# Two transformer layers on one core: the zero-padded queries made by DMA instead of by masked copies on VectorE, value matmuls of shifted copies listed one by one, and a newly planned order

## The chip, the cores and the metric

The kernel runs on one core of a Trainium2 chip. Five engines work side by side, each through its own list of instructions in the order written: TensorE (PE, matmuls), VectorE (DVE), ScalarE (ACT), GpSimd (POOL) and SyncE (SP, which issues the DMAs). They wait for each other by semaphores. The metric is the device time of one execution in microseconds (us); lower is better.

## The reference

Two layers, each an attention block and a dense block, over 2048 tokens of 512 numbers with 32 heads of 16. All data are bfloat16, and both layers use the same weights.

```python
def _A_ref(x, wqkv, wo):            # 32 heads, Dh = 16
    qkv = (x @ wqkv).reshape(B, S, 3, H, Dh)...
    scores = jnp.einsum("bhqd,bhkd->bhqk", q, k) * (Dh ** -0.5)
    p = softmax(scores)
    o = jnp.einsum("bhqk,bhkd->bhqd", p, v)
    return o.reshape(B, S, D) @ wo
def _B_ref(x, w1, b1, w2, b2):      # F = 1792
    return gelu(x @ w1 + b1) @ w2 + b2
x = x + _A_ref(layernorm(x), A_wqkv, A_wo)
x = x + _B_ref(layernorm(x), B_w1, B_b1, B_w2, B_b2)
# and both lines once more
```

Most of the work is in the scores: 2 layers x 32 heads x 2048 x 2048 exponentials, and the matmuls on both sides of them.

## The kernel before, in words

**Cells and passes.** The unit of attention is a cell: 128 keys by 512 query columns for one head (or, in the last two segments, 256 columns for each of two heads). A score matmul multiplies a 32-row slice of K (two heads of 16) with a 32-row slice of the padded query, `QP`, in which the 16 rows of the other head are zero. Slice a of four works on rows 32a to 32a+31 of TensorE, so up to four cells run at the same time. `passes` (L1211) cuts the 4096 cells into 96 passes: a pass is one padded query (half of the heads of a block of 128 rows, one segment of columns) with 16, 32, 48 or 64 cells. In the first layer the first segment's keys are taken in two parts, in the second layer those of the first two segments in three (`PARTS`, L50), which gives 24 passes of only 16 cells.

**Two ways to an exponential.** Most cells go to ACT: one ACTIVATE (L1751) takes two cells, sometimes three, from PSUM to the tiles `pt` (which, late or early, also lie in parts of K, Q, V and G that are free: these show up as `kt`, `q`, `v`, `g` at L1751). The others, at most those of 5 key tiles in 16 (`KD`), go to VectorE: one TENSOR_SCALAR (L1507) makes from the score a 16-bit word that, read as bfloat16, is roughly the exponential, and POOL makes three shifted copies of a pair of such cells with two integer adds (L1596 one copy, L1598 two). Each of the four copies is multiplied with its own scaled copy of V (`VC`) and all are added in PSUM: an exact enough exponential costs PE four value matmuls where one of ACT's cells costs one. Value matmuls (L1817) go in rounds of up to four, one for each column group a. The buffers `DU` of such pairs are few (5, and up to 5 lent ones).

**The padded query.** `QP` has three slots of 512 columns. `qpad` (L1288) makes one for each pass but the first: it waits for a slot, and VectorE multiplies the block of Q by a column of zeros and ones (L1299, 128x512 for most passes; two 128x256 ones for each of the last 8). The slot is given back when all scores of its pass have been handed out.

**Other work.** Loads of weights, `wr` (L1035), transposes of LayerNorm tiles by DMA (L778) and moves of x (L690) are all on SP's queue. VectorE also empties the projections from PSUM, adds residuals (L983, L1132), does LayerNorm (L734 to L774) and normalizes attention (L919 to L955). Projections and dense matmuls are L607.

**The order.** Nothing is ordered by hand. `_Sched` (L251) is a list scheduler that runs while the program is built: it keeps a clock for each engine, a cost for each operation, the time at which each result is ready (with a latency by engine, for a DMA a `tail`), and pools of buffers and PSUM banks. Generators yield operations; the one that can start first, or among those ready the one with the best priority, is taken, and the wait instructions follow from what it reads and writes. A VectorE operation marked as `port` starts, in the planner's eyes, only after the POOL operation that is running (`_ready`, L329), and POOL's after it. Whether a score group gets one more cell for VectorE is decided as PE's group is issued (`attach`, L1435): there must be a free bank, a free `DU` buffer, and VectorE's planned clock must not be too late. If none is attached, ACT may get a third cell (`extend`). Every 24 us of planned ACT time (`STRETCH`) ten settings of the planner are exchanged: `PICKS` names one of the rows of `ORDERS` for each stretch. Where PE would idle, it gets a filler matmul (L1339), and incomplete rounds get multiplications by zero (L1825).

Two places that a sentence cannot give are these, of the padded query and of the list of value matmuls (entries of `dq` are in the order in which PE will take them):

```python
s = yield ("acq", "qp")
for i, t in enumerate(ts):
    yield _Op("dve", 0.15 + 0.262 * w / 512, ... tensor_scalar(T["QP"][:, s, w*i:w*i+w], q, T["MASK"][:, t:t+1], 1.0, ...
...
yield _Op("pool", ..., words(2, 2), words(0, 2), 2 * SHIFT * ONES), ...)
self.chains -= 1
for jj, (pi, kt, a) in enumerate(cells):
    for i in range(4):
        self.dq[(pi, a)].append(...)
```

Of the kernel before, what the change touches and what calls it, by code (L numbers as in the profile page):

```python
# [27 lines left out]
QP_RING = 3  # L28
W_RING = 4
# [88 lines left out]
class _Prog:  # L118
# [72 lines left out]
    def group(self, eng, fns, reads=(), writes=(), sem=None, by=1):  # L191
        if sem is None:
            sem = ENG_SEM[eng]
        self._dep_waits(eng, reads, writes)
        for i, fn in enumerate(fns):
            last = i == len(fns) - 1
            self.prog[eng].append(("do", fn, sem if last else None, by if last else 0))
# [22 lines left out]
class _Op:  # L220
    __slots__ = ("eng", "cost", "fns", "reads", "writes", "sem", "by", "tail", "prio", "mode", "slack", "late", "back", "port", "limit", "after")

    def __init__(self, eng, cost, fns, reads=(), writes=(), sem=None, by=1, tail=0.0, prio=None, mode="F", slack=None):
        self.eng, self.cost = eng, cost
        self.fns = fns if isinstance(fns, list) else [fns]
        self.reads, self.writes = list(reads), list(writes)
        self.sem, self.by, self.tail, self.prio, self.mode, self.slack = sem, by, tail, prio, mode, slack
        self.limit = 1e9
        self.late, self.after = None, []
        self.port = eng == "dve" and self.writes[:1] != [] and self.writes[0].startswith(("OTT", "NMR", "QP", "VC", "XLN", "PT", "V0", "V1")) and not self.reads[:1] == [] and not self.reads[0].startswith("B.")  # L230
# [20 lines left out]
class _Sched:  # L251
# [23 lines left out]
    def route(self, name, what):  # L275
        return name
# [205 lines left out]
def bass_interleave_layers__mha_block__dense_activation_gelu__prompt_kernel(  # L482
# [15 lines left out]
    with ExitStack() as es:  # L498
# [28 lines left out]
        if DU % 2:  # L527
# [31 lines left out]
                     "dout", "dk0", "dk1"] + ["dwr%d" % i for i in range(W_RING + W_MORE)] + ["dtr%d" % i for i in range(XLN_RING)]  # L559
# [37 lines left out]
class _Plan:  # L597
# [12 lines left out]
    def init(self):  # L610
# [16 lines left out]
        yield _Op("dve", 0.6, lambda e: e.memset(self.bank(PVB), 0.0), writes=["B.%d" % PVB])  # L627
        yield _Op("dve", 0.1, lambda e: e.tensor_reduce(
# [170 lines left out]
    def proj(self, l, kind, i, c, src, skeys, ph, done):  # L799
# [43 lines left out]
        if (l, kind, i, c) == (0, "Q", 0, 0):  # L843
            s = yield ("acq", "qp")
            self.hold.add(b)
            yield _Op("dve", DV, lambda e: e.tensor_scalar(T["QP"][:, s, :], pb, T["MASK"][:, 0:1], None, op0=ALU.mult),
                      reads=["B.%d" % b, "MASK"], writes=["QP.%d" % s, "QFIRST"])
            first = ["QFIRST"]
            yield ("give", ("qp", 0), s)
# [437 lines left out]

    def qpad(self):  # L1288
        T = self.T
        for pi, (l, seg, g, kts, part, final) in enumerate(self.pas):  # L1290
            if pi == 0:
                continue
            b, ts = self.heads(seg, g)
            qc, q0, w = seg
            yield ("need", ("Q", l, b, qc))
            s = yield ("acq", "qp")
            q = T["Q"][:, b, 512 * qc + q0:512 * qc + q0 + w]
            for i, t in enumerate(ts):
                yield _Op("dve", 0.15 + 0.262 * w / 512, lambda e, s=s, q=q, i=i, t=t, w=w: e.tensor_scalar(  # L1299
                    T["QP"][:, s, w * i:w * i + w], q, T["MASK"][:, t:t + 1], 1.0, op0=ALU.mult, op1=ALU.mult),  # L1300
                    reads=["Q.%d.%d" % (b, qc), "MASK"], writes=["QP.%d" % s])
            yield ("give", ("qp", pi), s)
# [39 lines left out]
    def score(self, cell, qs, bank):  # L1342

        T = self.T
        pi, kt, a = cell
        l, seg, g = self.pas[pi][:3]
        gb = self.heads(seg, g)[0]
        lhsT = T["K"][l][32 * a:32 * a + 32, gb, kt * 128:(kt + 1) * 128]
        rhs = T["QP"][32 * a:32 * a + 32, qs, :]
        o = self.bank(bank)  # L1350
        return (lambda e: e.matmul(o, lhsT=lhsT, rhs=rhs, start=True, stop=True, tile_position=(32 * a, 0)),  # L1351
                ["K%d.%d.%d" % (l, gb, kt // 4), "QP.%d" % qs])
# [9 lines left out]
    def next_d(self, used, start, pop=True):  # L1362
        tok = self.s.tokens
        for pi in (self.pa, self.pa + 1):
# [12 lines left out]
            for k, (_, kt, a) in enumerate(self.dlist[pi]):  # L1377
                if a not in used and ("vc", l, kt) in tok and ("K", l, gb, kt // 4) in tok:
                    r = ["K%d.%d.%d" % (l, gb, kt // 4), "QP.%d" % tok[("qp", pi)]]
# [78 lines left out]
    def scores(self):  # L1458
        u = 0
        pools = self.s.pools  # L1460
        while True:
# [25 lines left out]
            for d, b, pair, j in extra:  # L1487
                yield ("spawn", self.dfirst(pair, j, b), DPRIO)
                if j == 0:
                    yield ("spawn", self.dchain(pair), CPRIO)  # L1490
# [14 lines left out]
    def dfirst(self, pair, j, b):  # L1505
        u = self.T["DU"][pair["du"]][:, 0, j, :]
        yield _Op("dve", 0.682, lambda e: e.tensor_scalar(u, self.bank(b), E_SCALE, E_BIAS, op0=ALU.mult, op1=ALU.add),  # L1507
                  reads=["B.%d" % b], writes=["DU.%d.0.%d" % (pair["du"], j)] + self.over(pair["du"]))
        pair["done"] = pair.get("done", 0) + 1
        yield ("rel", "dbank", b)  # L1510

    def solo(self):
# [10 lines left out]
        while True:  # L1523
# [10 lines left out]
            yield ("spawn", self.dfirst(pair, j, b), DPRIO)  # L1534
# [43 lines left out]
    def dchain(self, pair):  # L1578
# [9 lines left out]
        n = len(cells)  # L1588
        U = T["DU"][du]
        key = [["DU.%d.%d.%d" % (du, i, j) for j in range(n)] for i in range(4)]  # L1590
        def words(i, k):
# [5 lines left out]
                  reads=key[0], writes=key[1])  # L1597
        yield _Op("pool", 0.143 + 0.4352 * n, lambda e: e.int64_add(words(2, 2), words(0, 2), 2 * SHIFT * ONES),  # L1598
                  reads=key[0] + key[1], writes=key[2] + key[3])
        self.chains -= 1  # L1600
        self.duleft[du] = n
        for jj, (pi, kt, a) in enumerate(cells):
            l, seg, g = self.pas[pi][:3]
            gb, ts = self.heads(seg, g)
            j = KD[l].index(kt)
            for i in range(4):
                if i == 0:
                    ws, wk = [T["V"][l][:, kt, 8 * gb + 2 * a + t, 0:17] for t in ts], ["V%d.%d" % (l, kt), self.vone(l, kt)]
                else:
                    ws = [T["VC"][:, j, i - 1, 17 * h:17 * h + 17] for h in [8 * gb + 2 * a + t for t in ts]]  # L1610
                    wk = ["VC.%d.%d" % (j, i - 1)]
                self.dq[(pi, a)].append((ws, U[:, i, jj, :].bitcast(BF16), wk + [key[i][jj]],
                                         ("du", du) if i == 3 else None, i == 3, kt))
# [247 lines left out]
    def run(self):  # L1861
# [10 lines left out]
        s.pool("qp", range(QP_RING))  # L1872
# [54 lines left out]
```

## Time and profile before

| | |
|---|---|
| median of 3 runs | 1480.15 us (1477.9 to 1480.68) |
| the profiled execution | 1478.68 us |
| its span, first to last instruction | 1476.7 us |
| TensorE clock granted | 0.999 |
| VectorE exponents (L1507) | 858 + 200 + 115, mean 0.682 to 0.683 us |
| ACT exponentials (L1751) | 1164 of two cells, 198 of three, 1 of one |
| POOL adds (L1596, L1598) | 607 and 607 |
| masked copies (L1299) | 87 of 512 columns, 16 of 256 |
| DMA, all queues | 103.35 MB, 70 GB/s in the mean |

A row of the groups reads: line, engine, operation, what it writes and reads, shape, how many, then busy time and the mean of one in ns, then the idle time of the engine before them and who ended it. Busy time of ACT and PE counts overlapping instructions from start to end, so their steps are shorter than their durations. The windows' rows give the stretch in us, its length, then busy time and number for the engine asked, the granted clock, the DMA engines' share and GB/s.

### The profile page before, as it was taken

The page shows a single profiled execution, that of the slowest core. Times are in us where ns is not written, and L with a number is a line of the kernel's source. Part 1 is how long each engine was busy: PE and PEld are TensorE (multiplying, and loading weights), DVE is VectorE, ACT ScalarE, POOL GpSimd, SP SyncE. Part 2 cuts the span into 40 slices and gives each one's busy share as a digit, 9 for nine tenths or more (in the row PEclk, how much of TensorE's full clock was granted, in tenths as well). Part 3 has the DMA queues.
Part 4 walks back from the last instruction along what each step waited for, and adds up shares of the span by engine and source line. Part 5 has one row for each costly group of instructions (what it writes and reads, how often), then busy time and mean ns, then how long its engine had stood idle before and what let it go on. Part 6 is the DMA issues. An engine that isn't in the chain of part 4 may idle for free.

```text
span 1476.7 us, 45759 instructions
## 1 busy us (share of the span) xinstructions
PE 1415.5 (96%) x19639; PEld 428.0 (29%) x19639; DVE 1219.1 (83%) x2246; ACT 1427.6 (97%) x1422; POOL 977.8 (66%) x1235
## 2 busy tenths in 40 slices
PE   8999999999999999999999999999999999999999
PEld 3222222222222222222222222222222222334445
DVE  7768989878987789987797788999968987887683
ACT  7999999999999999999999999999999999999995
POOL 1057977867676777886556756667867876776661
PEclk9999999999999999999999999999999999999999
DMA  5200001153112521114320243101143115511533
GB/s 154 49 2 1 2 16 30 38 168 82 47 45 59 164 66 31 48 34 130 122 60 25 59 122 114 30 2 37 30 131 115 37 37 137 158 31 38 162 91 95
DMA packets 145045, 103.35 MB, mean 70 GB/s; under 512 B 37069, under 2 KB 143822, under 8 KB 144846
## 3 DMA queue, kind: packets, MB, share of 16 engines
q1 hardware_dynamic: 144846, 100.44, 24.6%
q8 instruction: 157, 2.57, 0.8%
q14 instruction: 42, 0.34, 0.1%
HBM read 88.61 MB, written 4.19 MB: 63 GB/s over the span
## 4 chain that ended last, share of the span: by engine, by line
ACT 52%; PE 30%; DVE 14%; DMA 1%; POOL 1%; issue 1%; SPq 0%; ACTq 0%; DVEq 0%
ACT pt L1751 41%; PE ps L607 10%; PE ps L1351 10%; PE ps L1817 9%; DVE du L1507 6%; ACT g L1102 3%; ACT kt L1751 2%; ACT q L1751 2%; ACT v L1751 2%; DVE kt L1507 1%; DVE v L1507 1%; DVE xln L774 1%; DVE stats L734 1%; DMA wr<-in_B_w_dram 1%; ACT L1102 1%
## 5 line engine op out<-in xcount | busy, mean ns | idle before, releaser
L1751 ACT ACTIVATE pt<-ps 128x1024 bf16<-128x1024 f32 (+1 forms) x1096 | 1103.9, 1136 | 18.2 <-PE ps L1351 12.0
L1507 DVE TENSOR_SCALAR du<-ps 128x512 uint16<-128x512 f32 x858 | 572.4, 683 | 115.9 <-PE ps L1351 112.3
L1351 PE MATMUL ps<-qp,kt 32*128 32x512 bf16 x4096 | 553.8, 384 | 37.4 <-ACT pt L1751 11.4
L1596 POOL INT64_ADD du<-du x444 | 266.9, 602 | 318.5 <-DVE du L1507 290.9
L1598 POOL INT64_ADD du<-du x444 | 449.1, 1013 | 35.5
L1817 PE MATMUL ps<-du,vc 128*17 128x512 bf16 (+1 forms) x2856 | 324.2, 360 | 1.4 <-ACT pt L1751 0.5
L1351 PEld LDWEIGHTS ps<-qp,kt 32*128 32x128 bf16 x4096 | 144.7, 91 | 601.3 <-issue 175.0
L1817 PE MATMUL ps<-pt,v 128*17 128x512 bf16 (+1 forms) x2630 | 283.9, 360 | 5.3 <-ACT pt L1751 2.1
L1507 DVE TENSOR_SCALAR kt<-ps 128x512 uint16<-128x512 f32 x200 | 134.7, 682 | 34.0 <-PE ps L1351 33.2
L1817 PE MATMUL ps<-du,v 128*17 128x512 bf16 (+1 forms) x952 | 142.4, 360 | 3.9 <-DVE xt L937 1.2
L1817 PE MATMUL ps<-kt,vc 128*17 128x512 bf16 (+1 forms) x714 | 136.3, 347 | 0.1
L607 PE MATMUL ps<-xf,wr 128*32 128x512 bf16 (+1 forms) x1888 | 131.0, 365 | 0.0
L607 PE MATMUL ps<-wr,g 128*32 128x512 bf16 x1600 | 118.9, 382 | 1.6 <-DMA wr<-in_B_w_dram 1.5
L1598 POOL INT64_ADD kt<-kt x104 | 105.1, 1011 | 8.3
L1817 PEld LDWEIGHTS ps<-du,vc 128*17 128x17 bf16 x2856 | 87.7, 89 | 75.3 <-issue 38.1
L1596 POOL INT64_ADD kt<-kt x104 | 62.4, 600 | 60.8 <-DVE kt L1507 57.4
L1817 PEld LDWEIGHTS ps<-pt,v 128*17 128x17 bf16 x2630 | 69.1, 88 | 87.7 <-issue 62.5
L1817 PE MATMUL ps<-v,vc 128*17 128x512 bf16 (+1 forms) x402 | 90.3, 350 | 0.0
L1081 DVE TENSOR_SCALAR g<-ps,hb1t 128x512 bf16<-128x512 f32 (+1 forms) x112 | 79.2, 708 | 12.7 <-PE ps L607 12.0
L1817 PE MATMUL ps<-kt,v 128*17 128x512 bf16 (+1 forms) x390 | 85.9, 360 | 1.6 <-DVE xt L937 1.3
L1507 DVE TENSOR_SCALAR v<-ps 128x512 uint16<-128x512 f32 x115 | 77.5, 682 | 11.9 <-PE ps L1351 11.6
L1751 ACT ACTIVATE kt<-ps 128x1024 bf16<-128x1024 f32 (+1 forms) x71 | 78.5, 1134 | 2.5 <-PE ps L1351 0.6
(108 smaller groups left out, 1555.4 us busy)
## 6 DMA issues: line engine op xcount, KB each, us to landing
wr<-in_B_w_dram SPq DMA_DIRECT2D x256, 256.0 KB, 2.9
wr<-in_A_wqkv_dram SPq DMA_DIRECT2D x24, 256.0 KB, 2.9
wr<-in_A_wo_dram SPq DMA_DIRECT2D x18, 256.0 KB, 3.1
x<-in_A_x_dram SPq DMA_DIRECT2D x7, 512.0 KB, 4.1
kept<-x SPq DMA_DIRECT2D x4, 512.0 KB, 2.9
x<-kept SPq DMA_DIRECT2D x4, 512.0 KB, 4.1
out_dram<-x SPq DMA_DIRECT2D x16, 128.0 KB, 2.6
g<-in_A_wqkv_dram SPq DMA_DIRECT2D x3, 512.0 KB, 6.0
```

Source lines behind the costliest of these rows:

```text
L607: return [lambda e, a=a: e.matmul(out[32 * a:32 * a + 32, :], lhsT=lhsT[:, 32 * a:32 * a + 32], rhs=rhs, start=start, stop=stop, tile_posi ...
L734: yield _Op("dve", 0.66, lambda e, t=t: e.bn_stats(T["STATS"][:, t, :], T["X"][:, t % XT, :]), reads=["X.%d" % (t % XT)], writes=["ST.%d" ...
L774: yield _Op("dve", 0.41, lambda e: e.tensor_scalar(xl, T["X"][:, t % XT, :], T["RSTD"][:, t:t + 1], T["NMR"][:, t:t + 1], op0=ALU.mult, op ...
L1081: yield _Op("dve", 0.21 + n / 966, lambda e, fc=fc, pb=pb: e.tensor_scalar(T["G"][:, fc, q], pb, T["HB1T"][:, fc:fc + 1], None, op0=ALU.ad ...
L1102: lambda e, g=g: e.activation(out=g, in_=g, func=ACT.Gelu_apprx_tanh), reads=gk, writes=gk, prio=2)
L1351: return (lambda e: e.matmul(o, lhsT=lhsT, rhs=rhs, start=True, stop=True, tile_position=(32 * a, 0)), ["K%d.%d.%d" % (l, gb, kt // 4), "Q ...
L1507: yield _Op("dve", 0.682, lambda e: e.tensor_scalar(u, self.bank(b), E_SCALE, E_BIAS, op0=ALU.mult, op1=ALU.add), reads=["B.%d" % b], writ ...
L1596: yield _Op("pool", 0.151 + 0.2176 * n, lambda e: e.int64_add(words(1, 1), words(0, 1), SHIFT * ONES), reads=key[0], writes=key[1])
L1598: yield _Op("pool", 0.143 + 0.4352 * n, lambda e: e.int64_add(words(2, 2), words(0, 2), 2 * SHIFT * ONES), reads=key[0] + key[1], writes=k ...
L1751: yield _Op("act", 0.065 + 0.4267 * n, lambda e, src=src, dst=dst: e.activation(out=dst, in_=src, func=ACT.Exp, scale=0.25), reads=["B.%d" ...
L1817: op.fns.append(lambda e, o=o, lhsT=q[0][0][m], rhs=q[0][1][:, n * m:n * m + n], a=a, st=st, sp=sp: e.matmul(o, lhsT=lhsT, rhs=rhs, start= ...
```

## The change

The wide masked copies are replaced by four DMAs on SP for each pass, 16 rows by 512 columns each, from `Q` into `QP`; the zero rows are written once at the start by a memset. For that a slot may only ever hold the same half: `QP` gets four slots, two for even and two for odd passes, each with a semaphore of its own (all four DMAs count on it, 64 in all). Keys for reads and writes are now kept for each slice a. The 256-column segments keep their copies on VectorE. Entries for value matmuls are appended singly, the unshifted copy when the exponent has been handed out, the shifted ones after each POOL add, where before all followed the second add. Small LayerNorm operations are marked as `port`, so that the planner counts on their waiting for POOL. `PICKS` is new.

```diff
-QP_RING = 3
+QP_RING = 4
...
-PICKS = (3, 9, 9, 3, 3, 3, 9, 3, 1, 3, 3, 9, 9, 9, 1, 9, 9, 3, 9, 9, 5, 3, 3, 9,
-         3, 9, 9, 9, 3, 1, 9, 9, 3, 9, 9, 9, 3, 3, 9, 3, 9, 3, 9, 9, 3, 5, 9, 5,
-         1, 9, 9, 9, 9, 3, 9, 9, 5, 3, 4, 3)
+PICKS = (3, 3, 3, 1, 3, 3, 1, 3, 4, 3, 3, 1, 3, 1, 3, 3, 4, 4, 3, 1, 3, 3, 1, 1,
+         3, 1, 1, 3, 3, 1, 1, 1, 1, 5, 1, 7, 1, 5, 3, 3, 5, 8, 3, 1, 9, 1, 1, 1,
+         3, 3, 3, 1, 3, 3, 1, 7, 3, 3, 4, 3)
...
+        spread = sem not in ENG_SEM and len(fns) > 1
...
+            if spread:
+                self.prog[eng].append(("do", fn, sem, by // len(fns)))
...
-... self.writes[0].startswith(("OTT", "NMR", "QP", "VC", "XLN", "PT", "V0", "V1")) ...
+... self.writes[0].startswith(("OTT", "NMR", "QP", "VC", "XLN", "PT", "V0", "V1", "VARR", "RSTD", "RA", "RB")) ...
...
+        yield _Op("dve", 0.5, lambda e: e.memset(T["QP"][:, 1:QP_RING, :], 0.0), writes=[k for i in range(1, QP_RING) for k in self.qkeys(i)])
...
+        if name == "qp":
+            return "qp%d" % (b % 2)
...
-            s = yield ("acq", "qp")
+            s = yield ("acq", "qp%d" % (pi % 2))
             q = T["Q"][:, b, 512 * qc + q0:512 * qc + q0 + w]
-            for i, t in enumerate(ts):
+            if w == 512:
+                fns = []
+                for a in range(4):
+                    rows = slice(32 * a + 16 * ts[0], 32 * a + 16 * ts[0] + 16)
+                    fns.append(lambda e, s=s, q=q, rows=rows: e.dma_start(T["QP"][rows, s, :], q[rows, :]))
+                yield _Op("sp", 1.6, fns, reads=["Q.%d.%d" % (b, qc)], writes=self.qkeys(s), sem="dqp%d" % s, by=64, tail=2.0)
+            for i, t in enumerate(ts) if w < 512 else ():
...
-    def dfirst(self, pair, j, b):
+    def dfirst(self, cell, pair, j, b):
...
+        self.copied(cell, pair["du"], j, 0)
...
+        self.duleft[du] = n
...
             reads=key[0], writes=key[1])
+        for jj in range(n):
+            self.copied(cells[jj], du, jj, 1)
...
             reads=key[0] + key[1], writes=key[2] + key[3])
+        for i in (2, 3):
+            for jj in range(n):
+                self.copied(cells[jj], du, jj, i)
         self.chains -= 1
-        self.duleft[du] = n
-        for jj, (pi, kt, a) in enumerate(cells):
...
+    def copied(self, cell, du, jj, i):
...
+        if i == 0:
+            ws, wk = [T["V"][l][:, kt, h, 0:17] for h in hs], ["V%d.%d" % (l, kt), self.vone(l, kt)]
+        else:
+            j = KD[l].index(kt)
+            ws, wk = [T["VC"][:, j, i - 1, 17 * h:17 * h + 17] for h in hs], ["VC.%d.%d" % (j, i - 1)]
+        self.dq[(pi, a)].append((ws, T["DU"][du][:, i, jj, :].bitcast(BF16), wk + ["DU.%d.%d.%d" % (du, i, jj)],
+                                 ("du", du) if i == 3 else None, i == 3, kt))
...
-        s.pool("qp", range(QP_RING))
+        s.pool("qp0", range(0, QP_RING, 2))
+        s.pool("qp1", range(1, QP_RING, 2))
```

More of the change, by code (lines that the diff above doesn't have):

```diff
@@ L229, in __init__ @@
         self.late, self.after = None, []
-        self.port = eng == "dve" and self.writes[:1] != [] and self.writes[0].startswith(("OTT", "NMR", "QP", "VC", "XLN", "PT", "V0", "V1")) and not self.reads[:1] == [] and not self.reads[0].startswith("B.")
+        self.port = eng == "dve" and self.writes[:1] != [] and self.writes[0].startswith(("OTT", "NMR", "QP", "VC", "XLN", "PT", "V0", "V1", "VARR", "RSTD", "RA", "RB")) and not self.reads[:1] == [] and not self.reads[0].startswith("B.")
 class _Thread:
@@ L558, in bass_interleave_layers__mha_block__dense_activation_gelu__prompt_kernel @@
         sem_names = ["pe", "act", "dve", "pool", "dxt0", "dxt1", "dxt2", "dxt3", "dx1", "dx2", "dx3", "dwq", "dwk", "dwv", "db1", "db2"] + ["dw%d" % c for c in range(3)] + [
-                     "dout", "dk0", "dk1"] + ["dwr%d" % i for i in range(W_RING + W_MORE)] + ["dtr%d" % i for i in range(XLN_RING)]
+                     "dout", "dk0", "dk1"] + ["dwr%d" % i for i in range(W_RING + W_MORE)] + ["dtr%d" % i for i in range(XLN_RING)] + ["dqp%d" % i for i in range(QP_RING)]
         sems = {n: es.enter_context(nc.semaphore("s_" + n)) for n in sem_names}
@@ L1286, in vcopies, with qkeys @@
             self.lend = 1
+    def qkeys(self, s):
+        return ["QP.%d.%d" % (s, a) for a in range(4)]
     def qpad(self):
@@ L1487, in scores @@
             for d, b, pair, j in extra:
-                yield ("spawn", self.dfirst(pair, j, b), DPRIO)
+                yield ("spawn", self.dfirst(d, pair, j, b), DPRIO)
                 if j == 0:
@@ L1533, in solo @@
             d, b, pair, j = extra[0]
-            yield ("spawn", self.dfirst(pair, j, b), DPRIO)
+            yield ("spawn", self.dfirst(d, pair, j, b), DPRIO)
             if j == 0:
```

28 lines of the change are left out of this document (12 added, 16 removed).

## The prediction

> **What bounds the kernel now.** I read the page first, for the engines' totals and the chain of work that ended last.
>
> ```profile
> span 1476.7 us, 45759 instructions
> PE 1415.5 (96%) x19639; PEld 428.0 (29%) x19639; DVE 1219.1 (83%) x2246; ACT 1427.6 (97%) x1422; POOL 977.8 (66%) x1235
> ...
> ACT 52%; PE 30%; DVE 14%; DMA 1%; POOL 1%; issue 1%; SPq 0%; ACTq 0%; DVEq 0%
> ...
> L1751 ACT ACTIVATE pt<-ps 128x1024 bf16<-128x1024 f32 (+1 forms) x1096 | 1103.9, 1136 | 18.2 <-PE ps L1351 12.0
> L1507 DVE TENSOR_SCALAR du<-ps 128x512 uint16<-128x512 f32 x858 | 572.4, 683 | 115.9 <-PE ps L1351 112.3
> ```
>
> ACT, PE and DVE all look full, so the question is which of them is out of work last. The chain of waits in order of time gives ACT's true rate, because successive exponentials overlap in the busy column:
>
> ```profile
> 195.31 2.27 ACT kt L1751 x2
> ...
> 224.83 1.15 DVE qp L1299
> ...
> 434.08 6.42 ACT pt L1751 x7
> ```
>
> Seven exponentials of two cells take 6.42 us, 0.917 each; a three-cell one shows 1.34 to 1.35 where it stands alone. Split by shape, the trace has 1164 pairs, 198 triples and one single: 1164 x 0.917 + 198 x 1.34 = 1333 us. With the gelus (47 us), the table loads (21) and small copies (14) ACT needs 1415 of 1476.7 us. The remaining 60 or so are mostly the 12.6 us ahead of the first exponential, the end after the last score (1448 us on), and waits for scores. The view of ACT's waits puts 12.0 us on PE's score matmuls in 24 waits. So **ACT is the bound**, and its work shrinks only if a cell (one head group by 128 keys) goes to VectorE instead: 2328 + 594 + 1 cells are ACT's, 858 + 200 + 115 = 1173 are VectorE's (the three L1507 groups), 4096 together. The code allows VectorE 5 of 16 key tiles, 1280 cells; 107 are still open.
>
> Where are they missing? The exponents on VectorE (L1507) by stretches of 60 us, and then the masked copies (L1299) in the same view:
>
> ```profile
> 720.00:780.00 60.00, 25.39 (x38) 1.00 0.26 67
> 840.00:900.00 60.00, 29.37 (x44) 1.00 0.46 133
> 900.00:960.00 60.00, 29.76 (x44) 1.00 0.18 50
> ...
> 840.00:900.00 60.00, 3.12 (x8) 1.00 0.46 133
> 900.00:960.00 60.00, 5.41 (x11) 1.00 0.18 50
> ```
>
> Most stretches hold 50 to 60 exponents, about the allowed share; seven after the start hold fewer (360, 720, 840, 900, 960, 1320, 1380 us: 48, 38, 44, 44, 43, 46, 49). Those seven hold 16.7 us of masked copies, 14.7 of it ahead of the 256-column segments, because the second layer's first passes are short and each pass makes one.
>
> **The change, part by part.**
>
> (1) *The masked copies leave VectorE.* By shape and from the view of the line itself:
>
> ```profile
> L1299 DVE TENSOR_SCALAR qp<-q,mask 128x512 bf16<-128x512 bf16 x87 | 39.8, 457 | 9.0 <-PE ps L1351 8.9
> ...
> L1299 DVE TENSOR_SCALAR qp<-q,mask x103: 268/344/1222, 13.3 to 1386.2; 128x512 bf16<-128x512 bf16 x87, 128x256 bf16<-128x256 bf16 x16
> ...
> 712.74 1.21 DVE L1299 TENSOR_SCALAR qp<-q,mask 128x512 bf16<-128x512 bf16 x1
> 712.76 1.04 POOL L1598 INT64_ADD du<-du  x1
> ```
>
> The 87 wide ones go, 87 x 0.457 = 39.8 us; the 16 of the two 256-column segments stay (7.4 us). The median is 0.344 and the longest 1.222: at 712.74 the copy lasts until the POOL add beside it ends, so it waits for that add. What is it worth? Bounds: nothing, if the planner finds no cell for the freed time, and 39.8 / 0.60 = 66 cells if all of it is refilled (0.60 is VectorE's back-to-back step per exponent in the chain at 211 to 224 us). I take the short stretches: 14.7 / 0.60 = 24 cells, since elsewhere the share of cells is at its limit. Each cell saves half a pair on ACT, 0.459 us: **-11 us** (bounds 0 and -30). PE does not lose by it: such a cell needs four value matmuls for one, three quarters of a 0.213 us round more (rounds of four columns follow each other at 0.21 in the timeline), 0.16 us; and it saves half a score group, which from the steady loop at 700 us (0.865 us for one score group and two rounds) costs 0.865 - 0.43 = 0.43, so 0.22.
>
> (2) *The copies on the path.* Summed over the chain, masked copies hold it for 9.8 us in 17 pieces, five of them over 1 us, as at 224.83. There exponents, LayerNorm and residual adds follow each other at 0.6 us, so VectorE itself is next and gets its work earlier; in the other pieces the next score or POOL is late at once. I take a third, **-3** (bounds 0 and -9.8), the rest being in (1) already.
>
> (3) *Four DMAs per pass on SP.* 87 x 4 = 348 more issues against about 400 in the trace. Four x loads of 128 KB take 1.82 us to issue, 0.46 each, the one-row bias load 0.24; so 1.0 to 1.8 us per pass, under 160 us on a queue whose listed work is far less than the span. Landing: 128 KB loads take 2.2 us, 512 KB ones 4.1. So a padded Q is there 4 us after its slot is free, against 0.46 now. The cover: from the end of the copy to the pass's first score there are 5.9 to 10.7 us in the 24 passes of 16 cells (868 to 1003 us), 2.2 in the pass after them, 12 to 48 elsewhere, except 6.3 and 9.9 in the first two. The slot now frees one pass earlier (two slots for each parity instead of three for all), about 5.5 us more there. **0 us**; without the cover, some 4 us per pass. In the first pass the loads keep the DMA engines full until 16 us and its scores begin at 18 to 20. The weight loads behind the DMAs on SP have margin: PE waits for them 1.5 us in all (bound +3). Every first score now also waits for a DMA semaphore; with the data landed I take nothing.
>
> (4) *Value matmuls handed out singly.* The unshifted copy of a cell can be used when its exponent is made, not after both POOL adds (0.60 and 1.01 to 1.04 us). PE waits little for POOL (1.6 us with its array idle), and POOL holds the chain for 1% of the span, 15 us, nearly all of it from 146 to 161 us where POOL itself is the limit and nothing is gained. But rounds can be filled earlier and the exponents' buffers come free sooner: **-1** (bounds 0 and -8).
>
> (5) *Waits for POOL in the plan, and the new order.* The LayerNorm steps of two or four columns now count as held up by POOL. The shortest `ra` steps take 0.14 us, the mean of the 2-column ones is 0.391; 38 of each kind with the other steps give some 20 us over their minimum. Planning cannot abolish the waits, only place them: -1. All 60 stretches get new settings: ACT's waits between exponentials, about 50 us in all, are redealt, and I see nothing that gives the sign (bounds -10 and +10), 0.
>
> (6) *Start:* one memset of 1536 columns more on VectorE, near 0.5 us (L627 takes 0.485 for 512 float32), at a time when VectorE waits for x: 0.
>
> Sum: -11 - 3 + 0 - 1 - 1 = -16; against the profiled execution, 1478.68 (span 1476.7 and 2.0 around it), 1462.7. That execution lies 1.5 under the median of the runs, 1480.15, so against the median 1464.2. Rounded up, since (1) and (2) share time, I forecast **1465 us**, 1.0% faster.
>
> **A rule that speaks against it.** The shortest landing in the trace, 2.2 us, is for 128 KB; here each transfer has 16 KB. The Trainium skill, DMA: Bandwidth & Descriptors, Rules for kernel authors, says to coalesce small transfers, since under 64 KB one pays mostly overhead. By that rule four in a row would pay it four times; were they served one after another at 2.2 us, Q would land after 9 us, still inside 5.9 + 5.5 us of the shortest lead, so it bears on the second rival's chance and not on the sum.
>
> **The rivals.**
>
> *No room.* VectorE already runs 83% and idles only while it waits for scores (112 + 33 + 12 us); if banks and the 5-of-16 limit, not its time, decide, no cells move and only (2), (4) and (5) remain, with PE (30% of the chain) next: 1478.7 - 4 and up to the time before, so 1474 to 1481, point 1477. For it: most stretches are at the share. Against it: the short stretches coincide with the masked copies. 0.22.
>
> *Late queries, slower.* SP runs in order. A padded Q stands behind transposes of LayerNorm tiles, for whose inputs SP waits up to 14.9 us at a time, and behind weight loads that wait for PE up to 161 us when the order places them early. If the real machine lags the plan, Q lands after the pass has begun, PE stops at the first score with everything queued behind it, and ACT follows within one exponential. It decides from 5.9 + 5.5 = 11.4 us between a free slot and landing. At 13 us the 24 short passes would lose 1.6 us each, 38 us over them if none is made up; halved for what ACT and VectorE have in stock, +19, less the 4 of (2) and (4): about 1494. Against it: 4 us needed, 11.4 there. 0.10.
>
> *The new order is worse.* PE's and ACT's waits grow by more than the gain, +8 after the saving: 1487. 0.08.
>
> **How the numbers follow.** Forecast case 0.60, its own range 1449 to 1474; no room 0.22; late queries 0.10; worse order 0.08. About 0.2% (3 us) is what a measurement of this kernel can tell from no change. Faster by more, under 1477: all of the forecast case and half of "no room", 0.71; within: most of its other half, 0.10; slower: the last two cases and its end at 1481, 0.19. The range, to leave out two in ten at most, goes from 1446 (66 cells at the most would give 1450 and the redealt waits the rest) to 1484.
>
> **What would show it.** Right: no wide L1299 groups on VectorE; L1507 groups sum to about 1197 (1180 to 1235); fewer ACT pairs, ACT's waits unchanged; SP's q<-q transfers landing in 2 to 4 us; no DMA of qp among PE's releasers. Wrong: as many L1507 as before, or fewer; PE idle before L1351 released by a DMA; more ACT idle from L1351; PE's zero-fills (L1825, 313) growing. What would make the forecast wrong: VectorE's freed time ending as idle while it waits for scores.

## The result: 0.23% slower

The changed kernel takes 1482.74 us in the median of 14 runs (1482.08 to 1484.64), the kernel before, run beside it, 1479.22 us (14 runs): a ratio of 1.0023, 95% interval 1.0015 to 1.0031. The forecast was 1465 us. The profiled execution took 1482.37 us with a span of 1480.6 us, 3.9 us more than before's 1476.7; the granted clock is 0.997, against 0.999 (where it fell is told below).

The page of the changed kernel: span, engines, chain of waits, the two groups of exponentials (line, engine, operation, shape, how many, then busy time and mean ns, idle time ahead and what ended it), and the DMA row of the padded queries (how many, KB each, median us to landing).

```profile
span 1480.6 us, 46284 instructions
PE 1419.3 (96%) x19765; PEld 431.6 (29%) x19765; DVE 1198.7 (81%) x2171; ACT 1421.8 (96%) x1410; POOL 986.5 (67%) x1233
...
PE 45%; ACT 37%; DVE 13%; POOL 3%; DMA 1%; issue 1%; SPq 1%; ACTq 0%; POOLq 0%; DVEq 0%
...
L1775 ACT ACTIVATE pt<-ps 128x1024 bf16<-128x1024 f32 (+1 forms) x1093 | 1100.0, 1126 | 25.0 <-PE ps L1367 13.6
L1523 DVE TENSOR_SCALAR du<-ps 128x512 uint16<-128x512 f32 x865 | 573.2, 683 | 143.1 <-PE ps L1367 139.4
...
qp<-q SPq DMA_DIRECT2D x348, 16.0 KB, 1.8
```

Lines have moved: exponents on VectorE are L1523 (L1507 before), on ACT L1775 (L1751), scores L1367 (L1351), LayerNorm outputs `xln` L779 (L774), their transposes L783 (L778); the DMAs of padded queries are L1312. The copies are gone and VectorE is busy 20.4 us less, but its idle time ahead of the exponents that wait for scores has grown from 115.9 to 143.1 us in the `du` group. The three groups hold 865 + 202 + 117 = 1184 cells, 11 more than before, and ACT is busy 5.8 us less. In the chain ACT fell from 52% to 37% and PE rose from 30% to 45%: ACT is less often the one that is late.

Where did the time go? The trace gives the time of each of the 4096 score matmuls. I divide the span at the 256th and at the last of them. For all kernels of this study, in us (the column LN is the time from `varr`, the first small operation of a LayerNorm, to `nmr`, the last, summed over the 25 LayerNorm groups):

| kernel | median | ratio to before, 95% | 256th score | from there to the last | after the last | LN | cells on VectorE |
|---|---|---|---|---|---|---|---|
| before | 1479.22 | | 117.6 | 1330.1 | 29.0 | 113.9 | 1173 |
| after | 1482.74 | 1.0023 (1.0015 to 1.0031) | 123.2 | 1322.6 | 34.8 | 137.8 | 1184 |
| e1 | 1486.41 | 1.0049 (1.0033 to 1.0065) | 122.3 | 1333.3 | 29.0 | 113.1 | 1173 |
| e2 | 1490.18 | 1.0081 (1.0068 to 1.0094) | 118.4 | 1334.2 | 34.8 | 140.8 | 1184 |
| e3 | 1478.25 | 0.9993 (0.9983 to 1.0002) | 118.1 | 1323.6 | 34.8 | 138.6 | 1184 |
| e4 | 1498.23 | 1.0123 (1.0093 to 1.0153) | 117.8 | 1337.8 | 39.4 | 115.0 | 1169 |
| e5 | 1498.68 | 1.0126 (1.0097 to 1.0156) | 119.6 | 1328.7 | 49.6 | 152.9 | 1173 |
| e6 | 1492.09 | 1.0082 (1.0053 to 1.0111) | 120.9 | 1329.6 | 38.7 | 106.1 | 1165 |
| e7 | 1490.80 | 1.0071 (1.0048 to 1.0094) | 120.7 | 1332.4 | 35.9 | 103.2 | 1177 |
| e8 | 1477.35 | 0.9983 (0.9974 to 0.9993) | 120.5 | 1326.2 | 28.9 | 107.0 | 1175 |
| e9 | 1498.62 | 1.0127 (1.0106 to 1.0148) | 120.6 | 1350.3 | 28.9 | 108.9 | 1175 |
| e10 | 1485.63 | 1.0040 (1.0028 to 1.0051) | 121.5 | 1333.8 | 30.0 | 111.0 | 1169 |

So the change lost 5.6 us in the first 120, gained 7.5 in the long middle and lost 5.8 after the last score: +3.9. The last two belong together. At the 3840th score the changed kernel is still 2.4 us behind before, at the 4096th it is 1.9 ahead: near the end its dense matmuls have been left for later, and they follow after the last score (see "The end"). Over the middle and the end it gains 1.7 us, and the loss is that of the start.

**The start.** The chain of waits of the changed kernel (start, duration, what), from 22.21 us on:

```profile
22.21 0.59 SPq L1312
...
22.85 0.59 SPq L1312
...
23.48 1.31 SPq L783
...
24.84 3.79 DMA kt<-xln
...
28.66 0.41 DVE xln L779
29.07 0.61 DVE v L875
```

Eight DMAs of padded queries in a row, from 17.81 us on, stand on SP's queue ahead of a transpose of the first LayerNorm tiles. (Besides the 24 short passes of the second layer, the first eight passes of the first layer have only 16 cells each, so passes, and with them query DMAs, follow each other closely here too.) The transposes free the tiles for the next `xln`, behind that stands the emptying of V (L875), and PE's value matmuls wait for V. The timeline of the same stretch, with idle time and its releaser in brackets, shows who pays:

```profile
26.06 0.41 DVE L779 TENSOR_SCALAR xln<-x,rstd,nmr 128x512 bf16<-128x512 bf16 x1 [2.76 <-DMA kt<-xln]
...
28.66 0.41 DVE L779 TENSOR_SCALAR xln<-x,rstd,nmr 128x512 bf16<-128x512 bf16 x1 [2.18 <-DMA kt<-xln]
...
29.73 0.60 PE L1841 MATMUL ps<-pt,v 128*17 128x512 bf16 x4 [3.17 <-DVE v L875]
```

Before, with nothing between the transposes, the same `xln` waited less, and so did PE:

```profile
24.32 0.41 DVE L774 TENSOR_SCALAR xln<-x,rstd,nmr 128x512 bf16<-128x512 bf16 x1 [1.16 <-DMA kt<-xln]
25.61 0.41 DVE L774 TENSOR_SCALAR xln<-x,rstd,nmr 128x512 bf16<-128x512 bf16 x1 [0.88 <-DMA kt<-xln]
...
26.68 0.40 PE L1817 MATMUL ps<-pt,v 128*17 128x512 bf16 x4 [0.54 <-DVE v L870]
```

The wait is only half of the loss. Towards its end the granted clock of PE falls to 0.50, from 28.5 to 35.3 us. The windows of the changed kernel, and then one of e3, which has the same order on PE and the copies of the first seven passes back on VectorE (stretch, length, PE's busy us and number, clock, DMA share, GB/s):

```profile
28.00:30.00 2.00, 0.27 (x4) 0.63 0.12 25
30.00:32.00 2.00, 2.00 (x18) 0.50 0.36 75
```

```profile
30.00:32.00 2.00, 2.00 (x37) 1.00 0.39 135
```

Between 30 and 32 us a matmul lasts 0.60 to 0.63 us, in e3 0.38 to 0.39. Matmul for matmul, the changed kernel is 2.7 us behind e3 when the wait for V ends and 5.1 us when the clock is back. The five kernels whose first passes get their queries by DMA (after, e1, e5, e6, e7) all show this: one wait of PE of 2.7 to 3.3 us, and about its end 3.4 to 6.8 us at half the clock begin. The other seven show neither: their longest wait between 18 and 40 us is 0.48 to 0.56 us.

**The end.** Before, the chain into the last part is ACT's exponentials and then its gelu; PE's dense work follows:

```profile
1447.42 0.92 ACT v L1751
1448.33 0.49 ACT pt L1751
...
1448.84 1.28 ACT L1102
...
1450.13 1.71 ACT g L1102
```

After, it goes through VectorE and the last LayerNorm but one:

```profile
1435.47 2.39 DVE du L1523 x4
1437.87 0.38 DVE xln L779
...
1438.28 3.90 DMA xf<-xln
...
1442.42 0.40 PE ps L611 x8
```

The last `xln` stands behind a row of exponents and comes at 1437.8 us (1428.9 before), so more dense work is left when the scores are done. These are the matmuls of that layer's first dense product from the last score on, before and then after:

```profile
L607 PE MATMUL ps<-xf,wr 128*32 128x256 bf16 x116 | 4.4, 273 | 0.0
```

```profile
L611 PE MATMUL ps<-xf,wr 128*32 128x256 bf16 x268 | 8.8, 273 | 0.3 <-DVE g L1086 0.3
```

152 more are left. The chain of the changed kernel has 182 dense matmuls in 9.11 us, 0.05 each; by that an estimate for the 152 is 7.6 us, about what the middle seemed to gain. So the longer end is, by this estimate, in the main work moved from the middle, not a loss of its own. This place is the same in after, e2 and e3, whose instructions on PE, ACT and POOL have one order.

### The profile page after: what moved, and what is told of

The parts are those of the page before. It is cut to its first block, busy times and chain, and to the rows that moved or that the text cites. A ratio compares the mean times of both kernels' runs of the same rounds, so it can differ in the third digit from the quotient of the medians.

```text
span 1480.6 us, 46284 instructions
## 1 busy us (share of the span) xinstructions
PE 1419.3 (96%) x19765; PEld 431.6 (29%) x19765; DVE 1198.7 (81%) x2171; ACT 1421.8 (96%) x1410; POOL 986.5 (67%) x1233
## 4 chain that ended last, share of the span: by engine, by line
PE 45%; ACT 37%; DVE 13%; POOL 3%; DMA 1%; issue 1%; SPq 1%; ACTq 0%; POOLq 0%; DVEq 0%
ACT pt L1775 28%; PE ps L611 15%; PE ps L1367 14%; PE ps L1841 14%; DVE du L1523 5%; ACT g L1107 3%; ACT q L1775 2%; DVE kt L1523 1%; ACT kt L1775 1%; ACT g L1775 1%; POOL du L1618 1%; ACT v L1775 1%; DVE xln L779 1%; PE ps L1355 1%; DVE v L1523 1%; POOL du L1614 1%
## 5 line engine op out<-in xcount | busy, mean ns | idle before, releaser
L1775 ACT ACTIVATE pt<-ps 128x1024 bf16<-128x1024 f32 (+1 forms) x1093 | 1100.0, 1126 | 25.0 <-PE ps L1367 13.6
L1523 DVE TENSOR_SCALAR du<-ps 128x512 uint16<-128x512 f32 x865 | 573.2, 683 | 143.1 <-PE ps L1367 139.4
L1367 PE MATMUL ps<-qp,kt 32*128 32x512 bf16 x4096 | 547.1, 384 | 31.8 <-ACT pt L1775 13.5
L1841 PE MATMUL ps<-du,vc 128*17 128x512 bf16 (+1 forms) x2883 | 335.5, 360 | 1.7 <-POOL du L1618 0.7
L1841 PE MATMUL ps<-pt,v 128*17 128x512 bf16 (+1 forms) x2619 | 306.5, 361 | 7.9 <-DVE v L875 3.2
L1367 PEld LDWEIGHTS ps<-qp,kt 32*128 32x128 bf16 x4096 | 142.4, 91 | 585.9 <-issue 187.9
L1841 PE MATMUL ps<-du,v 128*17 128x512 bf16 (+1 forms) x961 | 155.1, 360 | 4.2 <-DVE xt L942 2.0
L1523 DVE TENSOR_SCALAR kt<-ps 128x512 uint16<-128x512 f32 x202 | 135.6, 682 | 26.0 <-PE ps L1367 25.4
L1841 PE MATMUL ps<-kt,vc 128*17 128x512 bf16 (+1 forms) x720 | 143.6, 349 | 0.2
L1841 PEld LDWEIGHTS ps<-pt,v 128*17 128x17 bf16 x2619 | 75.1, 88 | 91.9 <-issue 58.3
L1523 DVE TENSOR_SCALAR v<-ps 128x512 uint16<-128x512 f32 x117 | 78.7, 681 | 16.4 <-PE ps L1367 16.1
L1841 PE MATMUL ps<-kt,v 128*17 128x512 bf16 (+1 forms) x352 | 80.7, 361 | 0.8 <-DVE xt L942 0.4
L1775 ACT ACTIVATE q<-ps 128x1024 bf16<-128x1024 f32 (+1 forms) x71 | 76.8, 1134 | 0.1
```

Source lines behind the costliest of these rows:

```text
L1775: yield _Op("act", 0.065 + 0.4267 * n, lambda e, src=src, dst=dst: e.activation(out=dst, in_=src, func=ACT.Exp, scale=0.25), reads=["B.%d" ...
L1841: op.fns.append(lambda e, o=o, lhsT=q[0][0][m], rhs=q[0][1][:, n * m:n * m + n], a=a, st=st, sp=sp: e.matmul(o, lhsT=lhsT, rhs=rhs, start= ...
```

## The experiments

None of them leaves out computation. In e1, e2, e3 and e9 the planner still counts what the original program had, while another instruction is written out in its place; so the order on PE, ACT and POOL is that of the original, instruction for instruction.

### e1: before's order, the copies by DMA

```diff
# before.py; planned as the masked copy on VectorE, written out as four DMAs on SP
-                yield _Op("dve", ..., tensor_scalar(T["QP"][:, s, ...], q, T["MASK"]...))
+                fns = [dma_start(T["QP"][rows(a, t), pi % 4, :], q[rows(a, t), :]) for a in range(4)]
+                op.alt = ("sp", fns, "dqp%d" % (pi % 4), 64)
+                yield op
```

> The kernel before, with every instruction of TensorE, ScalarE and GpSimd in its old order and the same 1173 cells on VectorE; only the 87 wide masked copies are gone from VectorE and 348 DMAs stand on SP where the copies stood in the plan. Theory A (VectorE's freed time is worth what the masked copies held on the chain, and SP's queue costs only at the start, where the LayerNorm transposes stand behind the query DMAs): VectorE's busy time falls by 38 to 40 us, the 256th score comes 2 to 5 us later than the 117.6 us of before, the rest gains 3 to 8 us; 1472 to 1480. Theory B (the query DMAs do no harm, the loss of the changed kernel is all in its new order): the 256th score stays at 117 to 118 us and the time falls by 4 to 10 us, 1469 to 1475. Rival C (the DMAs disturb throughout): over 1481.

e1 has the fourth slot and the memset (0.70 us) as well.

Measured: 1486.41 us, 0.49% slower, over the 1481 us of rival C. The page of e1, its engines and the `du` group:

```profile
PE 1418.7 (96%) x19639; PEld 428.0 (29%) x19639; DVE 1192.2 (80%) x2160; ACT 1428.1 (96%) x1422; POOL 977.0 (66%) x1235
...
L1520 DVE TENSOR_SCALAR du<-ps 128x512 uint16<-128x512 f32 x858 | 572.6, 683 | 132.0 <-PE ps L1364 128.8
```

VectorE is busy 1219.1 - 1192.2 = 26.9 us less, not the 39.8 that the copies' durations sum to. In before's trace 10.4 us of the 39.8, a quarter, lie beside the VectorE instruction before or after, so that only 29.4 are theirs alone; the memset and somewhat longer LayerNorm steps make up the rest. The idle time of the `du` group rises from 115.9 to 132.0. With the order held, little is gained. The start costs 4.7 us, half of it at half the clock as in after; some 1.9 us come back between 40 and 560 us; 0.6 are lost near 720 us, 3.6 from 820 to 915 us, and 1.0 at 1009 us, where PE waits for a padded query, the only such wait in this run. Between 820 and 915 us the chain of waits shows this:

```profile
855.65 1.07 SPq L1312
856.76 2.90 DMA wr<-in_B_w_dram
859.70 0.61 PE ps L612 x8
```

A load of weights stands behind the queries' DMAs and PE waits for it; at 892 us the same happens again. PE's waits for `wr` are 3.6 us in all, 1.5 before. Of the 3.6 us lost in this stretch these waits are about half; another 1.1 us are lost while the clock is 0.5, from 909.5 us on for 3.4 us.

### e2 and e3: after's order, copies back on VectorE, all of them or those of passes 1 to 7

```diff
# after.py; planned as four DMAs, written out as one masked copy
-                yield _Op("sp", 1.6, fns, ...)
+                op = _Op("sp", 1.6, fns, ...)
+                if True:            # e3: if pi < 8:
+                    op.alt = ("dve", [tensor_scalar(T["QP"][:, s, 0:512], q, T["MASK"][:, ts[0]:ts[0] + 1], ...)], None, 1)
+                yield op
```

> The changed kernel in its own order, but all 87 wide copies made by VectorE again at the place in the plan where the DMAs stood. Theory A (the start is lost because transposes wait behind query DMAs on SP): the 256th score comes at 118 to 120 us instead of 123.2; what the copies cost VectorE afterwards, with an order that left no room for them, is 4 to 10 us over the later 3840 cells; total 1478 to 1488. Theory B (the order alone): the 256th score stays at 122 to 124 and the total rises by the copies' cost, 1486 to 1493.

> The changed kernel in its own order, only the copies of passes 1 to 7 on VectorE again, the other 80 stay DMAs. Theory A: the 256th score comes at 118 to 120 us instead of 123.2 and the whole time falls by as much, 1477 to 1480. Theory B (the start is lost by the order, not by SP's queue): no change within 0.2%, 1481 to 1484.

Measured: e2 1490.18 us, e3 1478.25 us. With only the first seven copies back (e3) the 256th score comes at 118.1 instead of 123.2 us, the rest stays within 1 us of after, and the median falls by 4.5 us: so 5.1 of the 5.6 us lost at the start come from the DMAs of the first passes on SP's queue, the wait and the half clock after it together. Theory A holds for e3. In the group of `xln`, after and then e3:

```profile
L779 DVE TENSOR_SCALAR xln<-x,rstd,nmr 128x512 bf16<-128x512 bf16 x60 | 33.2, 567 | 5.8 <-DMA kt<-xln 5.1 <-DVE nmr L762 0.3
```

```profile
L780 DVE TENSOR_SCALAR xln<-x,rstd,nmr 128x512 bf16<-128x512 bf16 x60 | 33.4, 571 | 1.9 <-DMA kt<-xln 1.2 <-DVE nmr L763 0.3
```

With all copies back (e2) the start is mended too, but from the 256th score to the last it takes 11.6 us more than after, and 10.6 more than e3. In an order planned without them the 80 copies that e2 has over e3 cost 10.6 us, 0.13 each, more than the 4 to 10 that were expected; in before's order (e1) taking them away gained some 2 us at most. A reading that fits both is that the planner fills the time that it believes it has; e9 looks for the same in another order.

### e4 to e7: programs and lists of settings crossed, and the LayerNorm marks undone

```diff
# e4: before.py with after's PICKS.   e5: after.py with before's PICKS.
# e6, e7: after.py without the new marks; e7 with before's PICKS as well
-   startswith(("OTT", "NMR", "QP", "VC", "XLN", "PT", "V0", "V1", "VARR", "RSTD", "RA", "RB"))
+   startswith(("OTT", "NMR", "QP", "VC", "XLN", "PT", "V0", "V1"))
```

> The kernel before with only the list PICKS of the changed kernel, so the plan is made anew. Theory A (a list of settings fits the one program it was chosen for; the level comes from that choice, not from where the copies are made): 10 to 20 us slower than before, 1489 to 1499, with fewer than 1173 cells on VectorE. Theory B (the new list is the better or worse one by itself, whatever the program): within 5 us of the changed kernel, 1478 to 1488.

> The changed kernel with the old list PICKS. Theory A: 15 to 30 us slower than the changed kernel, 1497 to 1512. Theory B: within 5 us of before, 1475 to 1485. Theory C (the change frees VectorE and that shows on any list): faster than the kernel before with the new list.

> The changed kernel with its own list, but the small LayerNorm operations no longer marked as waiting for POOL, so the plan is made anew. Theory D (the marks make the planner postpone LayerNorm chains, which on the chip wait for POOL no less): the time from the variance to the scale of a LayerNorm group, summed over the groups, falls from 138 us back to about 114, the waits in the small operations do not grow by more than 5 us; with a list not chosen for it 1485 to 1498. Rival E (the marks spare real waits): the small operations take over 55 us instead of 44, and the later 3840 scores take longer than 1340 us.

> The changed kernel without the marks and with the old list: the program before but for the DMAs and the single hand-out. Theory A: no gain from freed VectorE time; 1484 to 1495 with a start some 5 us late, cells on VectorE 1165 to 1180. Theory C (freed time helps as soon as the plan knows of it): with a list that is as good for it as for before, 1465 to 1475 and over 1190 cells. Theory D: the sum of the LayerNorm chains near 114 us as without marks.

Measured: 1498.23, 1498.68, 1492.09 and 1490.80 us. Exchanging the lists costs both programs some 16 to 19 us, most of it in the time after the last score (39.4 and 49.6 us against 29.0 and 34.8) and, for before, in the middle. Theory A holds in both. A list is worth more than all the rest of this change, and each of these two fits its own program only. So a comparison of two programs each on its own list compares two searches as well, and undoing one part on a list of the whole is blurred by the misfit: the marks cost 7.9 us by e5 against e7, and gain 9.4 by after against e6.

One thing the four show without that blur. The marks were to spare the small LayerNorm steps (`varr` to `nmr`) their waits for POOL. The sum of those steps' durations is 44.1 us with marks (after and e5) and 46.3 and 44.9 without (e6, e7; before 47.3): at most 3 us saved. But the time from `varr` to `nmr` is 137.8 and 152.9 us with marks, 106.1 and 103.2 without. The planner, told that each step waits for POOL, spreads them, up to 19.2 us for one group in after, where before's longest is 9.8. That is theory D; rival E, over 55 us in the small steps, does not hold.

### e8: marks undone, start kept, and a list searched for this program

```diff
# e6, and:
-            if w == 512:
+            if not (w < 512 or pi < 8):        # passes 1 to 7 planned with the copy on VectorE
...
-PICKS = (3, 3, 3, 1, 3, 3, 1, 3, ...
+PICKS = (3, 3, 9, 3, 5, 3, 9, 3, ...       # found on the planner's own clock
```

> After with three edits: the LayerNorm marks undone, passes 1 to 7 planned with a copy on VectorE instead of the four DMAs, and a list of settings searched for this program on the planner's own clock. No computation is left out. Theory 'fit': what separated the runs so far is whether the list was searched for the program. Then this kernel, searched like before and after were, is within 6 us of before (1474 to 1486), far under the two runs without marks on lists of other programs (1490.8 and 1492.1). Theory 'parts': copies made by DMA and single value matmuls are worth what the prediction took for them once the start and the marks are mended; then 1462 to 1470. Theory 'marks pay': without them the LayerNorm chains cost more wherever they stand; then 1488 to 1495 again. Under each, the 256th score matmul is at 117.5 to 118.5 us, since the copies of the first passes are on VectorE, and the LayerNorm chains from varr to nmr sum to 100 to 115 us.

Measured: 1477.35 us, 0.17% faster than before (ratio 0.9983, 0.9974 to 0.9993), 5.4 us faster than the change. It is the fastest kernel of the study, by an amount that lies at the edge of what can be told from no change. The first theory holds: a program with most of the copies by DMA and single value matmuls, on a list of its own, comes back to before's time, and not to the 1462 to 1470 that the parts were to bring. But e3, with the marks and after's list, is within 1 us of it, so what sets e8 apart from after is shown for the start alone; no effect of the marks is seen where each program has a list of its own. The time after the last score is before's again (28.9 us). One number was missed: the 256th score comes at 120.5 us, not at 118, though the copies of the first passes are on VectorE; where these 2 us go was not followed up. On the page of e8:

```profile
PE 1416.0 (96%) x19669; PEld 429.3 (29%) x19669; DVE 1190.8 (81%) x2169; ACT 1425.6 (97%) x1422; POOL 978.5 (66%) x1241
...
ACT 52%; PE 32%; DVE 12%; POOL 2%; DMA 1%; issue 1%; SPq 0%; ACTq 0%
```

ACT is again the bound, with 1425.6 us of work for 1427.6 before: two cells more on VectorE, 1175, are all that 80 vanished copies brought here.

### e9: e8's order, its 80 copies back on VectorE

```diff
# e8, with the edit of e2
```

> The order of e8, instruction for instruction on PE, ACT and POOL, with the 80 copies that it makes by DMA put on VectorE as they are handed out (the plan still counts them on SP). No computation is left out. Theory 'an order without room': the planner has filled VectorE's time in this order too, so the copies cost 8 to 13 us more than e8, as they cost 10.6 to 11.6 in the order of after. Theory 'that order only': the 11 us belonged to the order of after; then 0 to 5 us more than e8.

Measured: 1498.62 us, 21.3 us more than e8, so the sign was right and the size too small by half. All of it lies between the 256th and the last score (1326.2 to 1350.3), spread over all its parts. The copies in this order:

```profile
L1315 DVE TENSOR_SCALAR qp<-q,mask 128x512 bf16<-128x512 bf16 x80 | 43.1, 538 | 10.1 <-PE ps L1371 9.9
```

They cost 24.1 us in the span of the profiled execution, the slowest of four, and 21.3 in the median, 0.27 us each, against 0.13 in e2: the price of the same instruction is set by the order around it. 3.3 of the 24.1 us come between 1018.8 and 1035.3 us, where the clock is 0.5 for 17.1 us (in e8 for 6.8 near there); the fastest run of e9 is still 18 us above e8. In e2 and e9 a copy stands where the DMA was planned, and VectorE may reach it too early. That this is part of the price is not shown: the idle time ahead of the copies is 10.1 us here, and 9.0 ahead of the 87 in before's own order.

### e10: e8 without single value matmuls

```diff
# e8, with a list of its own, searched in the same way
-        self.copied(cell, pair["du"], j, 0)            # in dfirst
...
+        for jj in range(n):                            # all four after the second add, as before
+            for i in range(4):
+                self.copied(cells[jj], du, jj, i)
```

> e8 with the value matmuls of a cell on VectorE listed together after the second POOL add again, as before the change, and its own list of settings, searched in the same way and for the same time as e8's. No computation is left out. Theory 'singles are small' (the prediction's term of 1 us, and the planner's own clock gives 2 us): 1477 to 1483, that is within 6 us of e8, which a list searched anew can move by itself. Theory 'singles carry it': the early rounds are what keeps e8 at before's time in spite of the other parts; then 1488 or more. Under the first, VectorE's exponents number 1165 to 1180; under the second, PE's waits for POOL's L1618 exceed 6 us (1.6 us before the change).

Measured: 1485.63 us, 8.3 us above e8, between the two bands. The largest difference is in one place: the 256 scores up to the 3840th take 97.9 us here and 87.5 in e8. The 256 after them win back 5.4 us (87.9 and 93.3), and the rest loses 4.5 in the sum. PE waits 1.7 us for POOL's second add, as little as before the change, where more than 6 were expected if the singles carried the result. So this run does not price the singles: whether they or the new list made that stretch longer is open.

## Why the prediction was wrong

**(1) The masked copies: the step that failed most.** "87 x 0.457 = 39.8 us go" took durations for free time; in the same order 26.9 us came free (e1). "Seven short stretches coincide with the masked copies" was read as a cause. Only three of the seven (840 to 1020 us) hold many copies, 12.1 of the 16.7 us; the other four hold 0.7 to 1.9 us each, where the stretches that are not short hold 1.8 in the mean. After the change these seven (360, 720, 840, 900, 960, 1320 and 1380 us) hold 316 exponents, 312 before. Here are the first four in the changed kernel (stretch, length, busy us and number, clock, DMA share, GB/s); with 48, 38, 44 and 44 before, the copies were not what kept them short:

```profile
360.00:420.00 60.00, 28.62 (x43) 1.00 0.26 73
720.00:780.00 60.00, 22.57 (x35) 1.00 0.32 84
...
840.00:900.00 60.00, 30.24 (x46) 1.00 0.47 137
900.00:960.00 60.00, 29.78 (x46) 1.00 0.22 62
```

11 cells moved instead of 24: 11 x 0.459 = 5.0 us in place of 11, and ACT's busy time fell by 5.8. The freed time ended as idle time ahead of the exponents, while VectorE waits for scores. That is the rival "no room", which had 0.22; its argument, VectorE idle only for scores, was on the table and was set aside for the coincidence. Its range, 1474 to 1481 us, holds e3 (1478.25), the changed kernel with the start mended.

**(2) The copies on the path, -3.** Where the order is held, some 1.9 us were gained up to 560 us and none after (e1), so less than was put down for them. What stood behind each piece of the chain was not followed.

**(3) The DMAs on SP at 0: failed, in a place that was not looked at.** What was looked at held: in the changed kernel Q is never late. Four landings end 3.6 to 5.9 us after the first issue, at least 2.1 us ahead of the pass's first score, 8 to 15 us in most of the 24 short passes, and PE has no wait for a DMA of `qp` in the changed kernel (0.8 us once in e1). But the cover was asked for Q alone, not for what stands behind its DMAs on SP. An issue takes 0.6 us in the median, 2.4 us per pass (1.0 to 1.8 were taken), and a transpose of a LayerNorm tile behind it holds SP for another 1.2 to 1.3 us, which was not in the working at all. Nor does the planner know it: the code counts 1.6 us for the four and 0.3 for a transpose. At the start LayerNorm, projections and passes run together, and the transposes pay: 5.1 us, shown by e3. Of these 2.7 us are PE's wait for V and 2.4 the half clock that follows it, which no term and no rival of the prediction had. The bound "+3" for weight loads was real in before's order (PE's waits for them rose from 1.5 to 3.6 us, e1); in after's order PE has no such wait. "Late queries, slower" had the right queue and the wrong victim.

As to the rule that was weighed against the forecast, the Trainium skill (DMA: Bandwidth & Descriptors, Rules for kernel authors) has transfers under 64 KB pay mostly overhead. This case agrees: 16 KB land in 1.8 us where 128 KB took 2.2, and the issue takes 0.59 us in the chain above, where an x load of 512 KB took 0.58 in e3. But the landings of four transfers overlap, while their issues add up.

**(4) Singles, -1.** Not settled (e10). PE's waits for POOL were small before and are small after, as was said.

**(5) Marks -1, new order 0: open.** The marks saved 3 us of waiting in the small steps and stretched the LayerNorm chains by 24 us in sum. What that costs in time is open: undoing them gains 7.9 us on one list (e5, e7) and costs 9.4 on the other (after, e6), and e3 with them and e8 without them are within 1 us of each other. The bounds of 10 us either way for a new order were too narrow, since lists alone moved the two programs by 16 to 19.

**(6) The memset, 0:** 0.70 us at 1.5 us into the span, while VectorE has nothing else: right.

In the sum -16 became +3.9: +5.6 at the start, where the DMAs were put at 0, and -1.7 for all the rest, steps (1), (2), (4), (5) and a new order together, where -16 was forecast. The time is inside the range given, the sign was wrong. Both misses point the same way, so the time is in the range by the range's width and not because a mechanism was right.

## What to carry to other kernels

When work moves to a queue that runs in order, ask for the instructions behind it there, not only whether its own result is in time; at the start of a kernel, where phases overlap, the answer differs from the steady part. A wait of PE can cost more than its length: here 2.7 us of waiting were followed by half the clock, which cost 2.4 us more. Busy time taken off an engine is a gain only if something can be named that will fill it: with the order held it ended as idle time here, and durations that overlap others do not all come free. Where time is divided at some event, ask what work has moved across it. Where a planner's settings are searched for one program, judge a change with the order held (what it costs by itself) and with a search of its own, since settings of another program cost more than the change.

## What the runs showed of the hardware that was not expected

- About the end of a single wait of PE of 2.7 to 3.3 us, near 29 us, five kernels were granted half the clock for 3.4 to 6.8 us, and their matmuls of 512 columns lasted 0.60 to 0.63 us instead of 0.38. Seven kernels with waits of at most 0.56 us there kept the full clock.
- Issuing a DMA on SP takes 0.59 us in the median for 16 KB on 16 rows; x and kept transfers of 512 KB took 0.34 to 0.59 us. One DMA transpose holds the queue for 1.2 to 1.3 us. Four small transfers in a row cost their issues, 2.4 us, while their landings (1.8 us each) overlap.
- A masked copy on VectorE holds the engine for less than its duration: of 39.8 us in the sum of 87 copies 10.4 lie beside a neighbouring VectorE instruction (before).
